# A decode block on one core: where 256 rows of w2 travel, and how the output sum is laid out in PSUM

## The chip, the core and the metric

The kernel runs on one core of a Trainium2 chip. Its metric is the device time of one execution in microseconds. The median of four runs is 134.85 us (134.83 to 134.93). The core has a matrix engine (TensorE, called PE in the profile; its weight loads are listed apart as PEld), a vector engine (DVE), a scalar engine (ACT), GpSimd (POOL) and SyncE (SP), which here issues most of the transfers. Sixteen DMA engines carry the transfers from HBM to the on-chip memory (SBUF). PE writes its results to PSUM, from which DVE and ACT read them.

## What is computed

One token for each of two batch rows (B = 2, Sq = 1, width D = 576) goes through an attention block over a window of the caches and, beside it, through a two-layer block with a squared ReLU. Both results are added to the input. With Hq = 32 query heads, Hkv = 16 key heads, head size 128, a cache of 8192 positions and F = 4608:

```
W = min(4096, max(256, Sk // 4))          # 2048 positions
q = (x @ wq) -> [B, Hq, 1, 128]
scores = q . k[last W] * 128**-0.5 ;  p = softmax(scores) ;  o = p . v[last W]
A = o.reshape(B, 1, Hq*128) @ wo
h = xn @ w1 + b1 ;  r = max(h, 0) ;  Bout = (r*r) @ w2 + b2
out = x + A(xn) + Bout(xn)                # xn = layernorm(x)
```

All inputs and the output are bf16. An execution reads 53.62 MB from HBM, nearly all of it caches and weights, and writes 2304 bytes.

## The kernel before

The work is cut into 8 units (4 groups of four key heads, 2 batch rows). For each unit, PE transposes the keys, forms scores, and later multiplies with the values; DVE and ACT copy transposed keys out of PSUM and make the softmax. `step(u)` interleaves the transposes and scores of unit u with the value product of unit u − 2. The products with `wo` (`wo_acc`), the hidden layer (`mlp_h_block`, `mlp_h_end`) and the products with `w2` (`mlp_o`, `mlp_x`, `mlp_tail`) follow by the order of the program text: PE's instructions are kept in program order.

SP's queue carries all large transfers, in this order: the first keys, `wq`, then keys and values in turn, the first half of `wo`, `w1`, the last two value tiles, the second half of `wo` (`issue_wo`, L156), and `w2` (`issue_w2`, L164). A transfer with 128 rows is shared out to the 16 DMA engines, 8 rows each. The keys, the values and the first three `w2` tiles take turns in six buffers (`kvpool`).

`w2` has 4608 rows. The first three quarters of 1152 rows each are one tile of 9 blocks of 128 rows. Of the last quarter, 7 blocks (896 rows) come last in SP's queue, as three transfers of 4, 2 and 1 blocks (`W2P`, L510). The other 256 rows travel early on ACT's queue in small transfers, one or two at a time (`issue_w2x`, L181), called from `load_k` and `load_v`. `XS` (L74) says how they are cut: each entry is (rows of w2 on a partition, partitions, partitions of one transfer). Before, 96 rows go as 4 transfers of 8 partitions with 3456 bytes each, and 160 rows as 4 transfers of 5 partitions with 9216 bytes each. `mlp_x` (L491) multiplies them by the hidden values.

The output sum is kept in PSUM. `out_ps` (L265) has two groups of 288 columns, group i on the partitions from 32 i on; each batch row lies on one partition of a group (16 apart). `out_acc` (L268) issues two matmuls of 288 columns for a block of rows. The sum starts with x and b2 (L556), and takes in the first `wo` half (L571), the 256 early rows (L580), the second `wo` half (L583) and three quarters of `w2` (L584). Then DVE and ACT copy it to SBUF (`part`, L586 to L589) in four pieces of 144 columns. The last 7 blocks go to another PSUM tile, `tail_ps`, in four column groups of 144 columns (`mlp_tail`, L479), four matmuls to a block. One DVE addition of `tail_ps` and `part` gives `fin_sb` (L594), and ACT issues its transfer to HBM (L595). Matmuls are recorded at L107 and transposes at L110, the lines of two helpers.

Of the kernel before, what the change touches and what calls it, by code (L numbers as in the profile page):

```python
# [8 lines left out]
F32 = mybir.dt.float32  # L9
BF16 = mybir.dt.bfloat16  # L10
ACT = mybir.ActivationFunctionType
ALU = mybir.AluOpType
# [4 lines left out]
def kernel(  # L17
# [14 lines left out]
    nc = tc.nc  # L32
    P = 128
    B, Sq, D = A_x.shape
# [32 lines left out]
    NG4 = 4  # L67
# [3 lines left out]
    HW = F // NG4  # L71
    HB = HW // 3
    FR = HW // P
    XS = ((3, 32, 8), (8, 20, 5))  # L74
    FT = (HW - sum(r * p for r, p, _ in XS)) // P
    F3 = (NG4 - 1) * HW
    CX = [(r, FT, P) for r in range(FT)]
    FX = []
    for xr, xp, _ in XS:
        FX.append(F3 + FT * P + sum(m * n for m, n, _ in XS[:len(FX)]))  # L80
        CX += [(FX[-1] - F3 + r, xr, xp) for r in range(xr)]
    assert FX[-1] + XS[-1][0] * XS[-1][1] == F
    N3 = (NG4 - 1) * FR
# [2 lines left out]
    BS = 16  # L86
    MB = BS * (B - 1) + 1
    RM = 32 * (NG4 - 1) + MB
    OH = D // 2
    OQ = D // 4  # L90
    NP = NQ // 2
    WR = 2 * NC * Dh // P
# [3 lines left out]
    const = ctx.enter_context(tc.tile_pool(name="const", bufs=1))  # L96
# [7 lines left out]
    psum = ctx.enter_context(tc.tile_pool(name="psum", bufs=1, space=bass.MemoryType.PSUM))  # L104

    def matmul(*a, **k):
        tc.keep_in_program_order(nc.tensor.matmul(*a, **k))  # L107
# [7 lines left out]
    k_tiles, v_tiles, wq_tiles, w1_tiles, wo_tiles, w2_tiles = {}, {}, {}, {}, {}, {}  # L115
# [59 lines left out]

    const.tile([P, 96], F32, name="pad_0")
    w2x_sb = [const.tile([xp, xr * D], BF16, name=f"w2x_sb_{i}") for i, (xr, xp, _) in enumerate(XS)]
    const.tile([P, 24], F32, name="pad_1")
    x_parts = [(s, i) for s, (_, xp, xe) in enumerate(XS) for i in range(xp // xe)]

    def issue_w2x():  # L181
# [61 lines left out]
    for sg in range(S):  # L243
# [12 lines left out]
                          in_=own[:].unsqueeze(2).to_broadcast([P, NC, HQ // NC]))  # L256
    in_s = const.tile([P, NS], F32, name="in_s")
    nc.vector.tensor_reduce(out=in_s[:], in_=ident[:].rearrange("p (g s c) -> p s g c", s=NS, c=NC), axis=AX.XY,
                            op=ALU.add)
    far_h = const.tile([TH, P], BF16, name="far_h")  # L260
    nc.vector.tensor_scalar(out=far_h[:].rearrange("p (a h r) -> p a h r", h=TH, r=rep),
                            in0=ident[0:TH, 0:TH].unsqueeze(1).unsqueeze(3).to_broadcast([TH, P // NC, TH, rep]),
                            scalar1=BIG, scalar2=-BIG, op0=ALU.mult, op1=ALU.add)
    is_h = ident[0:TH, 0:TH].unsqueeze(1).to_broadcast([TH, NJJ * 32 // TH, TH])
    out_ps = psum.tile([32 + MB, OH], F32, tag="out", name="out_ps")  # L265
    nc.vector.memset(out_ps[:], 0.0)

    def out_acc(lhsT, rhs_of, start=False, stop=False):  # L268
        for i in range(2):
            matmul(out_ps[32 * i:32 * i + MB, :], lhsT=lhsT, rhs=rhs_of(i * OH, (i + 1) * OH),  # L270
                   start=start, stop=stop, skip_group_check=True)

    QZ = 2 * NC
    qz = const.tile([P, NQ, B, 2, 3 * QZ], BF16, name="qz")
# [150 lines left out]
    def wo_acc(tq):  # L425
        ws = wo_state.pop(tq)
        wo_sb = wo_tiles.pop(tq)
        for r in range(WR):
            out_acc(ws[:, r, :], lambda a, z: wo_sb[:, r, a:z])

    mlp = {}
# [38 lines left out]
    def mlp_o(g, r0, r1):  # L470
        w2_sb = w2_tiles.pop((g, r0))
        for r in range(r0, r1):
            o = (r - r0) * D
            out_acc(mlp["h"][:, g * FR + r, :], lambda a, z: w2_sb[:, o + a:o + z], stop=(g == NG4 - 2 and r == r1 - 1))

    part = const.tile([RM, OQ], F32, name="part")
    nc.gpsimd.memset(part[:], 0.0)

    def mlp_tail(r0, r1):  # L479
        w2_sb = w2_tiles.pop((NG4 - 1, r0))  # L480
        if r0 == 0:
            mlp["out"] = psum.tile([P, OQ], F32, tag="o", name="tail_ps")
            nc.vector.memset(mlp["out"][:], 0.0)
        for r in range(r0, r1):
            o = (r - r0) * D
            for i in range(4):
                matmul(mlp["out"][32 * i:32 * i + MB, :], lhsT=mlp["h"][:, (NG4 - 1) * FR + r, :],
                                 rhs=w2_sb[:, o + i * OQ:o + (i + 1) * OQ], start=(r == 0), stop=(r == FT - 1),
                                 skip_group_check=True, tile_position=(0, 32 * i))

    def mlp_x():  # L491
        i = FT
        for w, (xr, xp, _) in zip(w2x_sb, XS):
            for r in range(xr):
                out_acc(mlp["h"][0:xp, N3 + i, :], lambda a, z: w[:, r * D + a:r * D + z])
                i += 1
# [13 lines left out]
    W2P = [(0, 0, 9), (1, 0, 9), (2, 0, 9), (3, 0, 4), (3, 4, 6), (3, 6, 7)]  # L510
# [33 lines left out]
    for t in range(NT):  # L544
# [7 lines left out]
                          in_=ident[0:NG4, 0:NG4].unsqueeze(2).to_broadcast([NG4, NG4, 32]))  # L552
# [28 lines left out]
    pv_all(NU - 1)  # L581
    wo_sel(1)
    wo_acc(1)  # L583
    for w in W2P[:NG4 - 1]:  # L584
        mlp_o(*w)
    for i in range(4):  # L586
        cp = nc.scalar.copy if i // 2 else nc.vector.tensor_copy
        cp(out=part[32 * i:32 * i + MB, :],  # L588
           in_=out_ps[32 * (i // 2):32 * (i // 2) + MB, (i % 2) * OQ:(i % 2 + 1) * OQ])  # L589
    for w in W2P[NG4 - 1:]:  # L590
        mlp_tail(*w[1:])

    fin_sb = work.tile([RM, OQ], BF16, tag="fin", name="fin_sb")
    nc.vector.tensor_tensor(out=fin_sb[:], in0=mlp["out"][0:RM, :], in1=part[:], op=ALU.add)  # L594
    nc.scalar.dma_start(out=out2d.rearrange("b (q n) -> q b n", q=4), in_=fin_sb[0:RM:BS, :])  # L595


# [28 lines left out]
```

## Time and profile before

| what | value |
|---|---|
| median of four runs | 134.85 us |
| the profiled execution | 134.87 us, of which its span 133.1 us |
| mean clock granted to PE | 0.858 of full speed |
| DMA | 53.74 MB at a mean 404 GB/s |
| instructions of PE, PEld, DVE, ACT, POOL | 850, 850, 160, 65, 18 |
| queues | q1: SP's large transfers; q10: ACT's small ones; q8 and q14: instructions |

The span runs from the first to the last instruction of the core; 1.8 us of the execution's time lie around it. A group or timeline line gives start or busy time, engine, source line, operation, the tile written and the tiles read, shapes and counts; the bracket at its end is the idle time of the engine before it, with what ended it. A line of the windows gives, for one stretch of time, the busy microseconds and instruction counts of PE, PEld, DVE, ACT and POOL, the clock granted to PE, the mean busy share of the 16 DMA engines, and GB/s. The chain of waits is followed back from the last instruction, at each step to what released it. The ends of matmuls are modelled in this profile.

### The profile page before, as it was taken

How to read it: one execution, taken by the hardware profiler on the slowest of the kernel's cores; microseconds unless marked ns; L12 is line 12 of the kernel's file. 1: busy time of each engine (PE TensorE's matmuls, PEld its weight loads, DVE VectorE, ACT ScalarE, POOL GpSimd, SP SyncE). 2: the span in 40 equal slices, each digit the busy share in tenths (PEclk: the TensorE clock that was granted, in tenths of full speed). 3: DMA queues.
4: the chain of work that ended last, by engine and by line, in shares of the span. 5: the costliest groups of instructions: out<-in, count | busy, mean ns of one | idle time of the engine just before them, and what ended most of it. 6: DMA issues, size and time to landing. Idle time of an engine off the chain costs nothing.

```text
span 133.1 us, 2082 instructions
## 1 busy us (share of the span) xinstructions
PE 90.7 (68%) x850; PEld 54.2 (41%) x850; DVE 58.7 (44%) x160; ACT 46.9 (35%) x65; POOL 5.4 (4%) x18
## 2 busy tenths in 40 slices
PE   0069746968597378569497599779755485927980
PEld 0059314544363235336253346536422243314650
DVE  6724405263484564484467537457520423061010
ACT  5715503078284255165085154366120400000010
POOL 7000000010100100100100100010100000000000
PEclk9999995599999999999999757999998555555599
DMA  3999999999999999999999999999999999999940
GB/s 119 432 412 422 443 414 453 414 438 424 419 433 442 419 446 409 448 414 449 409 438 428 424 443 424 438 416 443 438 418 427 414 456 426 422 412 433 407 187 1
DMA packets 4458, 53.74 MB, mean 404 GB/s; under 512 B 551, under 2 KB 682, under 8 KB 1230
## 3 DMA queue, kind: packets, MB, share of 16 engines
q1 hardware_dynamic: 4320, 53.32, 94.3%
q10 hardware_dynamic: 130, 0.31, 0.6%
q8 instruction: 6, 0.10, 0.3%
q14 instruction: 2, 0.02, 0.0%
HBM read 53.62 MB, written 0.00 MB: 403 GB/s over the span
## 4 chain that ended last, share of the span: by engine, by line
DMA 92%; PE 3%; DVE 1%; SPq 1%; issue 0%; DVEq 0%
DMA v<-in_A_v_cache_dram 43%; DMA k<-in_A_k_cache_dram 20%; DMA w<-in_B_w_dram 17%; DMA wq<-in_A_wq_dram 12%; PE kT_ps L110 2%; PE o_ps L107 1%; SPq L128 0%; DVE kT L329 0%; SPq L135 0%; DVE o L386 0%; DVE o L388 0%; DVE fin_sb L594 0%; PE tail_ps L107 0%; DVEq L594 0%
## 5 line engine op out<-in xcount | busy, mean ns | idle before, releaser
L110 PE MATMUL kT_ps<-ident_f,k 128*128 128x128 f32 x256 | 41.3, 307 | 12.1 <-DMA k<-in_A_k_cache_dram 7.9
L110 PEld LDWEIGHTS kT_ps<-ident_f,k 128*128 128x128 f32 x256 | 32.2, 157 | 26.3 <-issue 12.0
L327 ACT COPY kT<-kT_ps 128x1024 bf16<-128x1024 bf16 x32 | 31.8, 1012 | 22.2 <-PE kT_ps L110 22.1
L329 DVE COPY kT<-kT_ps 128x1024 bf16<-128x1024 bf16 x32 | 21.8, 683 | 16.8 <-PE kT_ps L110 16.5
L107 PE MATMUL sc_ps<-kT,qz 128*32 128x512 bf16 x128 | 10.5, 414 | 5.8 <-DVE kT L329 5.8
L107 PE MATMUL o_ps<-v,pT 128*32 128x512 bf16 x128 | 12.0, 474 | 0.3 <-DMA v<-in_A_v_cache_dram 0.3
L359 ACT ACTIVATE p<-sc_ps,bias 128x512 bf16<-128x512 f32 x8 | 5.5, 687 | 17.9 <-DVE gown L355 17.9
L588 ACT COPY part<-out_ps 17x144 f32<-17x144 f32 x2 | 0.5, 268 | 24.4 <-DVE part L588 24.4
L348 DVE TENSOR_REDUCE m<-sc_ps 128x1 f32<-128x512 f32 x8 | 5.5, 692 | 7.2 <-PE sc_ps L107 7.2
L388 DVE SCALAR_TENSOR_TENSOR o<-o_ps,in_s,o 128x128 f32<-128x128 f32 x24 | 8.3, 347 | 0.5
L362 DVE STREAM_TRANSPOSE pT<-p 128x512 bf16<-128x512 bf16 x8 | 5.7, 710 | 6.4 <-ACT p L359 6.4
L386 DVE TENSOR_SCALAR o<-o_ps,in_s 128x128 f32<-128x128 f32 x8 | 2.7, 341 | 10.8 <-PE o_ps L107 10.8
L107 PE MATMUL out_ps<-wo,ws 128*17 128x288 bf16 x64 | 6.1, 364 | 1.6 <-DVE ws L421 1.6
L352 POOL PARTITION_ALL_REDUCE gmax<-m x8 | 2.9, 365 | 90.2 <-DVE m L350 90.2
L107 PE MATMUL op_ps<-o,of_h 128*128 128x129 f32 x16 | 4.0, 340 | 3.3 <-DVE o L388 3.2
L107 PEld LDWEIGHTS <-qz 128*32 128x32 bf16 x128 | 2.2, 98 | 10.0 <-DVE kT L329 7.4
L107 PEld LDWEIGHTS <-hT_sb 128*17 128x17 bf16 (+2 forms) x104 | 4.8, 105 | 3.5 <-issue 0.9
L107 PEld LDWEIGHTS <-xnT 128*2 128x2 bf16 x100 | 2.3, 85 | 9.5 <-issue 8.1
L107 PEld LDWEIGHTS <-ws 128*17 128x17 bf16 x64 | 3.6, 112 | 3.8 <-DVE ws L421 1.8
L110 PE MATMUL pro_ps<-ident,tmp_x 2*128 2x2 bf16 x6 | 0.5, 176 | 6.6 <-DVE tmp_x L233 6.6
L107 PEld LDWEIGHTS op_ps<-o,of_h 128*128 128x128 f32 x16 | 2.8, 220 | 5.4 <-DVE o L388 5.4
L107 PE MATMUL h_ps<-w,xnT 128*2 128x384 bf16 x48 | 2.7, 363 | 3.2 <-DMA w<-in_B_w_dram 3.2
(79 smaller groups left out, 58.2 us busy)
## 6 DMA issues: line engine op xcount, KB each, us to landing
k<-in_A_k_cache_dram SPq DMA_DIRECT2D x8, 2048.0 KB, 23.5
v<-in_A_v_cache_dram SPq DMA_DIRECT2D x8, 2048.0 KB
wo<-in_A_wo_dram SPq DMA_DIRECT2D x2, 2304.0 KB
w<-in_B_w_dram SPq DMA_DIRECT2D x2, 2304.0 KB
wq<-in_A_wq_dram SPq DMA_DIRECT2D x2, 2048.0 KB, 16.4
w<-in_B_w_dram SPq DMA_DIRECT2D x3, 1296.0 KB
w_rem<-in_B_w_dram SPq DMA_DIRECT2D x1, 576.0 KB, 36.6
w<-in_B_w_dram SPq DMA_DIRECT2D x1, 576.0 KB
```

The source lines that it names most:

```text
L107: tc.keep_in_program_order(nc.tensor.matmul(*a, **k))
L110: tc.keep_in_program_order(nc.tensor.transpose(*a, **k))
L327: nc.scalar.copy(out=kT, in_=kT_ps[:])
L329: nc.vector.tensor_copy(out=kT, in_=kT_ps[:])
L348: nc.vector.tensor_reduce(out=m1[:], in_=sc_ps[:], axis=AX.X, op=ALU.max)
L352: nc.gpsimd.partition_all_reduce(gmax[:], m2[:], channels=P, reduce_op=ReduceOp.max)
L359: nc.scalar.activation(out=p_sb[:], in_=sc_ps[:], func=ACT.Exp, bias=bias[:, 0:1], scale=scale, accum_out=o1[:, Dh:Dh + 1])
L362: nc.vector.transpose(out=pT[:].rearrange("p j r -> p (j r)"), in_=p_sb[:])
L386: nc.vector.tensor_scalar(scalar1=in_s[:, 0:1], scalar2=None, op0=ALU.mult, **kw)
L388: nc.vector.scalar_tensor_tensor(scalar=in_s[:, k:k + 1], in1=o1[:, 0:Dh], op0=ALU.mult, op1=ALU.add, **kw)
L588: cp(out=part[32 * i:32 * i + MB, :], in_=out_ps[32 * (i // 2):32 * (i // 2) + MB, (i % 2) * OQ:(i % 2 + 1) * OQ])
```

## The change

The 256 early rows are cut in another way. The 160 rows in transfers of 5 partitions with 9216 bytes stay and now come first; the other 96 rows become one transfer of 96 partitions with 1152 bytes each, which is shared out to all DMA engines. So ACT issues five such transfers in place of eight, and `mlp_x` has 9 blocks in place of 11.

`out_ps` now has four column groups of 144 columns from the start, and `out_acc` issues four matmuls of 144 columns for a block of rows. All blocks of `w2`, the last seven too, go through `mlp_o` into this one tile. `mlp_tail`, `tail_ps`, `part` and its four copies go away. One ACT copy takes the whole of `out_ps` to `fin_sb`. A padding tile in SBUF grows by 384 bytes on each partition.

```diff
-    XS = ((3, 32, 8), (8, 20, 5))
+    XS = ((8, 20, 5), (1, 96, 96))
...
-    const.tile([P, 24], F32, name="pad_1")
+    const.tile([P, 120], F32, name="pad_1")
...
-    out_ps = psum.tile([32 + MB, OH], F32, tag="out", name="out_ps")
+    out_ps = psum.tile([RM, OQ], F32, tag="out", name="out_ps")
     nc.vector.memset(out_ps[:], 0.0)
 
     def out_acc(lhsT, rhs_of, start=False, stop=False):
-        for i in range(2):
-            matmul(out_ps[32 * i:32 * i + MB, :], lhsT=lhsT, rhs=rhs_of(i * OH, (i + 1) * OH),
-                   start=start, stop=stop, skip_group_check=True)
+        for i in range(4):
+            matmul(out_ps[32 * i:32 * i + MB, :], lhsT=lhsT, rhs=rhs_of(i * OQ, (i + 1) * OQ), start=start, stop=stop,
+                   skip_group_check=True, tile_position=(0, 32 * i))
...
-            out_acc(mlp["h"][:, g * FR + r, :], lambda a, z: w2_sb[:, o + a:o + z], stop=(g == NG4 - 2 and r == r1 - 1))
-
-    part = const.tile([RM, OQ], F32, name="part")
-    nc.gpsimd.memset(part[:], 0.0)
-
-    def mlp_tail(r0, r1):
-        w2_sb = w2_tiles.pop((NG4 - 1, r0))
-        if r0 == 0:
-            mlp["out"] = psum.tile([P, OQ], F32, tag="o", name="tail_ps")
-            nc.vector.memset(mlp["out"][:], 0.0)
-        for r in range(r0, r1):
-            o = (r - r0) * D
-            for i in range(4):
-                matmul(mlp["out"][32 * i:32 * i + MB, :], lhsT=mlp["h"][:, (NG4 - 1) * FR + r, :],
-                                 rhs=w2_sb[:, o + i * OQ:o + (i + 1) * OQ], start=(r == 0), stop=(r == FT - 1),
-                                 skip_group_check=True, tile_position=(0, 32 * i))
+            out_acc(mlp["h"][:, g * FR + r, :], lambda a, z: w2_sb[:, o + a:o + z], stop=(g == NG4 - 1 and r == FT - 1))
...
-    for w in W2P[:NG4 - 1]:
+    for w in W2P:
         mlp_o(*w)
-    for i in range(4):
-        cp = nc.scalar.copy if i // 2 else nc.vector.tensor_copy
-        cp(out=part[32 * i:32 * i + MB, :],
-           in_=out_ps[32 * (i // 2):32 * (i // 2) + MB, (i % 2) * OQ:(i % 2 + 1) * OQ])
-    for w in W2P[NG4 - 1:]:
-        mlp_tail(*w[1:])
 
     fin_sb = work.tile([RM, OQ], BF16, tag="fin", name="fin_sb")
-    nc.vector.tensor_tensor(out=fin_sb[:], in0=mlp["out"][0:RM, :], in1=part[:], op=ALU.add)
+    nc.scalar.copy(out=fin_sb[:], in_=out_ps[:])
```

More of the change, by code (lines that the diff above doesn't have):

```diff
@@ L88 @@
     RM = 32 * (NG4 - 1) + MB
-    OH = D // 2
     OQ = D // 4
```

## The prediction

> **What bounds the kernel now.** I read the page first, then the chain of waits in order of time, the windows of the last microseconds, the timeline of the same stretch, and the records of single DMA packets under them (each with queue, size, start and duration).
>
> ```profile
> PE 90.7 (68%) x850; PEld 54.2 (41%) x850; DVE 58.7 (44%) x160; ACT 46.9 (35%) x65; POOL 5.4 (4%) x18
> ...
> q1 hardware_dynamic: 4320, 53.32, 94.3%
> q10 hardware_dynamic: 130, 0.31, 0.6%
> q8 instruction: 6, 0.10, 0.3%
> ...
> DMA 92%; PE 3%; DVE 1%; SPq 1%; issue 0%; DVEq 0%
> ```
>
> No compute engine is above 68%. The DMA engines carry 92% of the chain, and the DMA row of the page is at 9 tenths from the second slice to the thirty-eighth.
>
> ```profile
> 107.64 22.06 DMA w<-in_B_w_dram
> 129.70 0.04 issue
> 129.74 0.27 PE tail_ps L107 x4
> ...
> 130.08 0.31 DVE fin_sb L594
> ```
>
> This is the end of the chain: the last w2 transfer, four matmuls, one addition. The transfer does not end on all 16 DMA engines together:
>
> ```profile
> 127.70:128.20 0.50, 0.50 (x14) 0.39 (x10) 0.00 (x0) 0.00 (x0) 0.00 (x0) 1.00 0.62 238
> 128.20:128.70 0.50, 0.43 (x12) 0.12 (x10) 0.08 (x1) 0.00 (x0) 0.00 (x0) 1.00 0.38 141
> 128.90:129.20 0.30, 0.18 (x12) 0.03 (x1) 0.29 (x2) 0.00 (x0) 0.00 (x0) 1.00 0.13 46
> 129.20:129.40 0.20, 0.04 (x4) 0.04 (x7) 0.03 (x1) 0.06 (x1) 0.00 (x0) 1.00 0.07 23
> ```
>
> The last two columns are the DMA share and GB/s. 0.13 is two engines of 16, 0.07 is one. So the bound is the most loaded DMA engine, not the bytes. Chained by start and end, the packet records give 16 engines. They finish their w2 work between 126.53 and 129.40 us, and their order follows what else each carried:
> - no extra packet: about 126.5 to 127.0;
> - a q8 packet (16 KB of instructions, 0.88 to 0.97 us each): six engines, 128.0 to 128.6;
> - four w2x packets of 9216 B and four of 3456 B, which the change's wording calls engines 0 to 4: 128.52, 128.62, 128.77, 129.22 and 129.40. The last two also carry a q14 packet of 8 KB.
>
> For the last engine, start, extra packets and slow packets add up to 129.39, against 129.40 recorded.
>
> **The change part by part.**
>
> *The w2x rows.* On one engine a 3456 B packet takes 131 ns from start to start, a 1152 B packet 47, the closing 4 B write 5. Engines 0 to 4 keep the 9216 B packets, lose four transfers of one 3456 B packet (4 x 136 = 544 ns) and gain one share of the 96-row transfer (6 x 47 + 5 = 287): −0.257 us. Engines 5 to 7 change alike; engines 8 to 15 gain 0.287. The latest of those without 9216 B packets ends at 128.59, so at most at 128.88 after. The five become 128.26, 128.36, 128.52, 128.96 and 129.14. The last landing moves from 129.40 to 129.14. Bounds: −0.44 (if the other loads let 128.96 be last) and 0 (if some other load takes the gain back). I take −0.26, since the sum of the packets explains the last engine within 0.01 us.
>
> *Output in four column groups.* Per block of rows, two matmuls of 288 columns become four of 144.
>
> ```profile
> 120.51 4.01 PE L107 MATMUL out_ps<-wo,ws 128*17 128x288 bf16 x32 [1.55 <-DVE ws L421]
> ...
> 124.32 4.26 PE L107 MATMUL out_ps<-w,hT_sb 128*17 128x288 bf16 x54
> ...
> 128.65 0.43 PE L107 MATMUL tail_ps<-w,hT_sb 128*17 128x144 bf16 x16
> ```
>
> The tail already has the new form: four blocks start 62.5 ns apart at clock 1.00. In the old form blocks start 122 ns apart at clock 1.00 and 240 at 0.50, so I estimate the new form at 125 at 0.50. w2x goes from 11 blocks (2.64 us) to 9 (1.1), the second wo part from 4.0 to 2.0, each w2 tile of 9 blocks to 1.1. One w2 tile takes 8 x 385.5 ns = 3.08 us to arrive, so each is summed before the next is there: PE, now done at 128.58, waits on every landing instead. None of this is on the path; worth 0, as the last matmuls wait for the last landing before and after.
>
> The Trainium skill ("TensorEngine Tiling (Array Packing)", Instruction Overhead) speaks against more and smaller matmuls: about 60 cycles for each. By that rule the 134 added matmuls would be about 3.4 us at 2.4 GHz (an estimate from the page), still under the spare 2 us of each w2 tile; the tail's 16 matmuls in 0.43 us do not show it.
>
> *The clock at the end.* The clock came back from 0.50 to 1.00 at 125.92, after a window with PE busy throughout:
>
> ```profile
> 119.09:122.50 3.41, 1.99 (x18) 1.22 (x20) 1.26 (x4) 0.00 (x0) 0.00 (x0) 0.50 1.00 426
> 122.50:125.92 3.42, 3.42 (x32) 2.04 (x30) 0.00 (x0) 0.00 (x0) 0.00 (x0) 0.50 0.99 417
> ```
>
> With half the work PE is busy about 1.1 us of each 3.08, so I expect 0.50 to the end. A 288-column matmul at the head of a group took 282 ns at 1.00 and 412 at 0.50; 144 columns fewer is 60 ns less of that difference, so the last four matmuls take 0.07 longer: +0.07 (0 if the clock returns; above, +0.16, the growth of a queued one, 286 to 448).
>
> *One ACT copy.* The addition on DVE took 0.307 and began 0.103 after PE's end, as it waits for PE and for ACT's part copies (a separate waiting instruction, then the addition). The copy waits for PE alone; ACT copies after PE began 0.036 to 0.048 later. The part copies on ACT took 0.268 for the same 144 columns on 17 partitions, and I take that for 113, as 98 and 128 partitions of 1024 columns both took 1.012. Together −0.06 − 0.04 = −0.10. The output transfer follows DVE by 0.033 now; following ACT's own completion I take the same, between 0 and +0.1. It is queued on ACT behind the copy alone, and its other wait is for a transfer that landed long before.
>
> *Hidden or empty.* The four part copies (0.30 each on DVE, 0.27 on ACT) end at 129.88, under the wait for the last matmuls: 0. Two memsets go (0.22 on POOL at 2.8 us, 0.18 on DVE at 118.2): 0, under the DMA stream. ACT issues five w2x transfers instead of eight (0.63 to 0.76 each); their completions share a rotation of eight with SP's, and SP now waits on three of them. From SP's waits (us in total, times, longest):
>
> ```profile
> SPq L128 <- DMA w2x_sb<-in_B_w_dram: 16.2, 3, 14.1
> ```
>
> and the page's table of DMA issues (its last column is the time from issue to landing):
>
> ```profile
> k<-in_A_k_cache_dram SPq DMA_DIRECT2D x8, 2048.0 KB, 23.5
> ```
>
> A k transfer lands 23.5 us after its issue, so SP is several transfers ahead: moving these waits costs 0 unless that lead is used up. SP's order of transfers is unchanged. The early 9216 B packets delay engines 0 to 4 by 0.42 at about 6 us, under the same lead.
>
> *More instructions.* PE gets 264 more. The six q8 packets start about every 250 PE records (matmuls and weight loads), so one more is due, 0.9 us on one engine, while w2 arrives. Four of the six lie on engines without w2x packets, two on engines 5 to 7, each on another one; if the seventh goes to the next, it meets an engine at 126.5 to 127.0, which then ends near 128.2, hidden. The Trainium skill ("Runtime: NRT & Kernel Launch", Instruction fetch mechanics) says blocks of 16 KiB, 256 instructions, mostly hidden; it does not name the DMA engine.
>
> Sum against the profiled execution (134.87; span 133.1 and 1.8 around it; 0.02 above the median of 134.85): −0.26 − 0.10 + 0.07 = −0.29, 134.58 there, 134.56 against the median.
>
> **The rivals.**
> 1. The last engine does not move: slow packets at the start (they add up to 1.0 us on the last engine, 0.1 on the least) fall differently and eat 0.26. For: that spread. Against: runs within 0.1 us of each other. −0.10 + 0.07: 134.82.
> 2. Slower: the seventh instruction packet lands on one of engines 0 to 4. On the one ending at 129.14 it gives 130.06: +0.66 − 0.10 + 0.07 = +0.63, 135.48. It costs more than the rest gains from the engine now at 128.77 upwards, three of the five. Against: the six packets avoid these five.
> 3. PE becomes the bound: were the four groups to take turns, a block at 0.50 would be 480 ns, a w2 tile 4.3 us against 3.08 of arrival, and three tiles end about 4 us late: 138.5. Against: the tail's rows.
> 4. More gain: the clock is back at 1.00 (134.49), or a q14 packet falls elsewhere and 128.96 is last: 134.38.
>
> **How the numbers follow.** The sum as forecast has 0.55 (134.45 to 134.70), rival 1 0.17, rival 2 0.11, rival 3 0.03, rival 4 0.14. The range leaves out rivals 2 and 3 and a part of the edges: 134.36 to 134.92. A difference under 0.2% (0.27 us) is about what a measurement of this kernel can't tell from none, and the forecast lies at that edge, 134.58: faster takes two thirds of the first case and all of rival 4 (0.50), within 0.2% the rest of it and nearly all of rival 1 (0.34), slower rivals 2 and 3 with a tail of 1 (0.16).
>
> **What would show it.** In the windows the last DMA share goes to zero at about 129.14 instead of 129.40; the output sums show three separate bursts of 36 matmuls with waits for w2 between; the clock is 0.50 in the last windows; the copy starts under 0.05 after PE and takes 0.27; q8 counts 7 packets. The prediction is wrong if the DMA share lasts beyond 129.3, if PE is still busy with a w2 tile when the next lands, or if the copy or the output transfer waits for something else.

## The result and the profile after

The changed kernel takes 134.75 us (median; 134.55 to 134.89) against 134.86 (134.76 to 135.18) for the kernel before on the same chips. The ratio is 0.9989 with a 95% interval of 0.9984 to 0.9993, so 0.15 us less, between 0.09 and 0.22. That is a real gain, but within 0.2%. The forecast of 134.56 lies 0.19 below the median; the range from 134.36 to 134.92 holds it. Some executions of kernels below took longer, up to 140.6 us, and in the three of these that were traced the 16 KB packets were 0.07 us slower over part of the run; the ratios leave out executions from 136.9 us up, the ranges given show them all.

The profiled execution of the changed kernel took 134.55 us, at the lower edge of its spread, while the one of before, at 134.87, lay in the middle of its own. So the two traces differ by 0.32 us, twice what the ratio gives. This matters below: the trace after shows what the change can do, and other executions have to show what it does as a rule.

From the page after (the span; engines with busy time, share and instructions; DMA queues with packets, MB and share of 16 engines):

```profile
span 132.8 us, 2335 instructions
PE 86.0 (65%) x982; PEld 52.5 (40%) x982; DVE 57.2 (43%) x156; ACT 46.6 (35%) x64; POOL 5.2 (4%) x17
...
q1 hardware_dynamic: 4320, 53.32, 94.6%
q10 hardware_dynamic: 178, 0.31, 0.6%
q8 instruction: 7, 0.11, 0.3%
```

PE has more instructions and less busy time. The small queue q10 carries the same bytes in more packets, and there is a seventh instruction packet on q8.

The end of the chain of waits after (start, duration, what):

```profile
101.19 27.20 DMA w<-in_B_w_dram
128.39 0.04 issue
128.43 0.66 PE out_ps L106 x16
129.09 0.04 issue
129.13 0.71 PE out_ps L106 x12
129.84 0.02 issue
129.86 0.28 ACT fin_sb L572
```

The addition on DVE is gone; one ACT copy follows PE by 0.046 us (from the unrounded records). The x12 group from 129.13 hides the last wait inside it: its last four matmuls wait for the last landing, as the windows after show (the last two columns are the DMA share and GB/s, the one before them the clock granted to PE):

```profile
127.70:128.20 0.50, 0.50 (x21) 0.40 (x13) 0.00 (x0) 0.00 (x0) 0.00 (x0) 0.50 0.75 284
128.20:128.70 0.50, 0.37 (x16) 0.27 (x15) 0.00 (x0) 0.00 (x0) 0.00 (x0) 0.50 0.42 152
...
128.90:129.20 0.30, 0.26 (x12) 0.07 (x7) 0.00 (x0) 0.00 (x0) 0.00 (x0) 0.50 0.07 23
129.20:129.40 0.20, 0.20 (x8) 0.14 (x8) 0.00 (x0) 0.00 (x0) 0.00 (x0) 0.50 0.00 0
```

Nothing moves after 129.20; before, one engine was still busy in the last of these stretches. The clock is 0.50 to the end, where it was 1.00. The timeline after shows why:

```profile
118.88 2.10 PE L106 MATMUL out_ps<-wo,ws 128*17 128x144 bf16 x64 [1.55 <-DVE ws L420]
120.85 1.26 PE L106 MATMUL out_ps<-w,hT_sb 128*17 128x144 bf16 x36
123.94 1.26 PE L106 MATMUL out_ps<-w,hT_sb 128*17 128x144 bf16 x36 [1.83 <-DMA w<-in_B_w_dram]
127.04 2.77 PE L106 MATMUL out_ps<-w,hT_sb 128*17 128x144 bf16 x64 [1.84 <-DMA w<-in_B_w_dram]
129.86 0.28 ACT L572 CAST fin_sb<-out_ps 113x144 bf16<-113x144 f32 x1 [24.56 <-PE out_ps L106]
```

A `w2` tile of nine blocks is summed in 1.26 us, and PE then waits 1.8 us for the next one. Before, PE ran through this stretch without a pause.

The path of the end can be split by the records of packets, matmuls and completions. All values are in us; "landing" is the end of the last packet of the last `w2` transfer (PE is released about 0.3 later), "issue" is when ACT starts to issue the output transfer, and what lies around the span is the time less the span.

| execution | landing | to issue | issue to span's end | around the span | time |
|---|---|---|---|---|---|
| before | 129.40 | 1.03 | 2.66 | 1.79 | 134.87 |
| after | 129.17 | 1.00 | 2.59 | 1.79 | 134.55 |
| difference | −0.23 | −0.03 | −0.07 | 0 | −0.32 |

### The profile page after: what moved, and what is told of

Its sections match the earlier page's. It is cut to its first block, busy times and chain, and to the rows that moved or that the text cites. A ratio compares the mean times of both kernels' runs of the same rounds, so it can differ in the third digit from the quotient of the medians.

```text
span 132.8 us, 2335 instructions
## 1 busy us (share of the span) xinstructions
PE 86.0 (65%) x982; PEld 52.5 (40%) x982; DVE 57.2 (43%) x156; ACT 46.6 (35%) x64; POOL 5.2 (4%) x17
## 4 chain that ended last, share of the span: by engine, by line
DMA 77%; PE 16%; SPq 2%; DVE 2%; issue 1%; ACT 0%; DVEq 0%
DMA w<-in_B_w_dram 47%; DMA k<-in_A_k_cache_dram 17%; DMA wq<-in_A_wq_dram 13%; PE kT_ps L109 8%; PE sc_ps L106 3%; PE q_ps L106 2%; PE o_ps L106 1%; PE out_ps L106 1%; DVE qrow L292 1%; SPq L127 1%; SPq L134 1%; PE qT_ps L109 1%; DVE kT L328 1%; DVE qz L308 0%; SPq L158 0%
## 5 line engine op out<-in xcount | busy, mean ns | idle before, releaser
L109 PE MATMUL kT_ps<-ident_f,k 128*128 128x128 f32 x256 | 39.8, 300 | 11.0 <-DMA k<-in_A_k_cache_dram 7.7
L109 PEld LDWEIGHTS kT_ps<-ident_f,k 128*128 128x128 f32 x256 | 30.7, 152 | 25.2 <-issue 11.6
L106 PEld LDWEIGHTS <-xnT 128*2 128x2 bf16 x100 | 2.8, 100 | 12.9 <-issue 12.1
L106 PE MATMUL out_ps<-w,hT_sb 128*17 128x144 bf16 x136 | 5.1, 319 | 3.8 <-DMA w<-in_B_w_dram 3.7
L106 PE MATMUL h_ps<-w,xnT 128*2 128x384 bf16 x48 | 3.2, 421 | 5.8 <-DMA w<-in_B_w_dram 5.8
L452 DVE TENSOR_TENSOR hrow<-t 98x384 bf16<-98x384 f32 x3 | 1.6, 557 | 8.3 <-ACT t L451 8.2
L106 PE MATMUL q_ps<-wq,xnT 128*2 128x512 bf16 x32 | 2.7, 477 | 3.2 <-DMA wq<-in_A_wq_dram 3.2
```

Of the source, the lines that this page charges most:

```text
L109: tc.keep_in_program_order(nc.tensor.transpose(*a, **k))
L452: nc.vector.tensor_tensor(out=hrow[:, k * HB:(k + 1) * HB], in0=t1, in1=t1, op=ALU.mult)
```

## The experiments

**1. Each part alone.** The first kernel takes the new cut of the rows into the kernel before:

```diff
-    XS = ((3, 32, 8), (8, 20, 5))
+    XS = ((8, 20, 5), (1, 96, 96))
...
-    const.tile([P, 24], F32, name="pad_1")
+    const.tile([P, 616], F32, name="pad_1")
```

> Only the new cut of the 256 early rows, on the kernel before. First theory: the end follows the DMA engine that lands last, and the cut takes 0.26 us from it: about 134.60, last landing near 129.14 in the trace, clock back at 1.00 at the end. Rival A (the column groups or the ACT copy cost more than the 0.03 gain that was forecast for them together): the same 134.60 here. Rival B (the gain of the rows is itself eaten in most executions, by loads on the DMA engines that differ from one execution to the next): about 134.75, with a wider spread than the kernel before.

Measured: 134.67 us (134.53 to 134.82), ratio 0.9984 (0.9976 to 0.9993), so −0.21 us between −0.32 and −0.09. The end of its chain of waits:

```profile
107.38 22.08 DMA w<-in_B_w_dram
129.46 0.04 issue
129.50 0.27 PE tail_ps L107 x4
129.77 0.04 DVEq L594
129.80 0.05 issue
129.85 0.31 DVE fin_sb L594
```

Before, the same chain had the four matmuls at 129.74, so they move by 0.24. The end keeps its old form: four matmuls in 0.27, then the addition, 1.03 us from landing to issue. The rows alone bring the whole gain. Part of it, 0.08, lies behind the issue of the output: from there to the span's end it is 2.58 in this trace, where it was 2.66.

The second kernel has the four column groups and the ACT copy with the old cut of the rows:

```diff
-    XS = ((8, 20, 5), (1, 96, 96))
+    XS = ((3, 32, 8), (8, 20, 5))
...
-    const.tile([P, 120], F32, name="pad_1")
+    const.tile([P, 168], F32, name="pad_1")
```

> Only the four column groups and the ACT copy, with the old cut of the early rows. First theory and rival B: 0.10 less after the last matmul, 0.07 more for the slower clock, so 134.83, last landing at 129.40 as before. Rival A: 134.97 or more, as the whole change gained some 0.15 less than forecast.

Measured: 135.08 us (134.78 to 136.04), ratio 1.0026 (1.0008 to 1.0044): slower by 0.35 us, and not by what lies on the path. The landing of its trace, 129.36, and the 1.00 us to issue are as forecast, but the time around the span was 1.78 to 3.04 us from execution to execution, where it is 1.8 in the kernels above. This cost does not appear in the changed kernel, so it needed a cause of its own (experiment 4).

**2. The whole change again, and before again.** The changed kernel ran beside the two parts, which gave a second trace of it; then each kernel ran once more, for a third trace of the changed one and a second of the one before.

> The changed kernel once more, for a second trace. First theory: the same order of engines as in the first trace, last landing 129.17, time within 0.05 of 134.55. Rival B: a time nearer to 134.75, and a last landing later by the same amount, with a load on the last engine that the first trace does not show there.

Measured: 134.70 us (134.53 to 134.82), ratio 0.9987 (0.9978 to 0.9995). On the same chip the rows alone took 134.67, so the groups and the copy add nothing that shows. Its last landing was at 129.20.

> The changed kernel, a third trace. The two traces so far are of executions at 134.55 and 134.61, the median is 134.70 to 134.75. First theory: the last landing between 129.15 and 129.35, on an engine that carries four packets of 9216 B and one 8 KB instruction packet, and the time 5.4 us after it. Rival B: another engine last, or another load on it.

> The kernel before, a second trace. First theory: last landing near 129.40, on an engine with the same packets as in its first trace. Rival B: a last landing that differs from the first by 0.1 us or more, with slow packets at the start to account for it.

Measured: 134.91 us for the changed kernel and 134.89 for the one before. The second trace of before repeats the first: landing 129.40, 1.03 to issue. The third trace of the changed kernel does not repeat its first; its windows are

```profile
128.90:129.20 0.30, 0.30 (x16) 0.30 (x11) 0.00 (x0) 0.00 (x0) 0.00 (x0) 0.50 0.09 31
129.20:129.40 0.20, 0.20 (x11) 0.04 (x1) 0.00 (x0) 0.00 (x0) 0.00 (x0) 0.50 0.06 23
129.40:129.60 0.20, 0.17 (x12) 0.11 (x8) 0.00 (x0) 0.00 (x0) 0.00 (x0) 0.50 0.03 12
```

and the end of its chain is

```profile
129.48 0.70 PE out_ps L106 x12
130.18 0.02 issue
130.21 0.28 ACT fin_sb L572
```

One engine is at work until 129.52, 0.35 later than in the first trace after (129.17), and the time is 0.36 longer. Everything behind the landing is the same: 0.99 to issue, 2.60 from there. So the difference between these traces is that of the last landing; in the second trace, too, the landing (129.20) and the time (134.61) lie 0.03 and 0.06 above the first. The packet records of the engine that ends last show a stall of 295 ns right behind its second 9216 B packet, at 9.37 us. No such stall stands on the last engine in the first trace after. The stall is not the whole difference: added up packet by packet, this engine is 0.27 later than in the first trace by 12 us, and it loses another 0.07 between 50 and 56 us, where the packets of the 96-row transfer lie. In the run of the rows alone, the second-last engine stalls for 209 ns at the same place, at 9.95 us; in the two traces of before, whose packets there have 3456 B, the largest single stall is 132 ns. But in the second of them the losses between 8 and 12 us add up to 0.22 on each of the last two engines, so losses there do not come with 9216 B packets alone.

**3. The same rows at another time, and in other cuts.** If the early 9216 B packets cost time on engines 0 to 4, sending them later should recover it. Here the first two calls of `issue_w2x` send nothing. All five transfers move by this: the first 9216 B packets leave at about 31 us instead of 5.6, and the 96-row transfer travels at 59 to 63 us instead of 50 to 55:

```diff
+    x_calls = []
+
     def issue_w2x():
-        if x_parts:
+        x_calls.append(0)
+        if x_parts and len(x_calls) > 2:
             s, i = x_parts.pop(0)
```

> The changed kernel with the first two early-row transfers issued later: the calls at the start of the program issue nothing, so the first 9216 B packets come at about 32 us instead of 5.6 and 9 us. Theory C, from three traces of the changed kernel (last landing 129.17, 129.20, 129.52): in some executions the packets next to the early 9216 B ones stall for 0.2 to 0.7 us at 9 to 11 us, on the very engines that end last, and that takes back a part of the 0.26. Then: last landing near 129.15 in nearly every execution, median about 134.58, spread narrower than 0.3. Rival: the stalls at the start come anyway and fall on other packets: 134.70, spread as before.

Measured: 134.52 us (134.45 to 134.70, and one execution of 140.2), ratio 0.9977 (0.9968 to 0.9986), so −0.31 us between −0.43 and −0.19. Every execution but that one has a span of 132.7 to 132.9. Windows and end of the chain:

```profile
128.90:129.20 0.30, 0.25 (x12) 0.15 (x8) 0.00 (x0) 0.00 (x0) 0.00 (x0) 0.50 0.04 12
129.20:129.40 0.20, 0.20 (x8) 0.06 (x1) 0.00 (x0) 0.00 (x0) 0.00 (x0) 0.50 0.00 0
```

```profile
102.44 26.57 DMA w<-in_B_w_dram
129.00 0.04 issue
129.05 0.71 PE out_ps L106 x10
129.75 0.02 issue
129.78 0.28 ACT fin_sb L575
```

The last landing is at 129.08. This kernel is faster than both. It gains 0.16 us more than the change did (0.31 − 0.15), with an uncertainty of about 0.14 from the two intervals, so the difference is shown, but not its exact size, and not which of the moved transfers brings it. The early packets are one candidate; what they do at 9 to 11 us is read from single traces, and in this one the last engine loses nothing there, but neither does it in the first two traces of the changed kernel. The 96-row transfer is the other. On the engine that ends last it took longer than its own packets need, by 0.09, 0.14 and 0.16 us in the three traces of the changed kernel and by 0.08 with the rows alone; here, at 59 to 63 us, by 0.02. No run moved one without the other.

The next kernel spreads all but 80 of the rows over all engines, which gives many small packets:

```diff
-    XS = ((8, 20, 5), (1, 96, 96))
+    XS = ((8, 10, 5), (1, 96, 96), (1, 80, 80))
...
```

> The changed kernel with 80 rows on engines 0 to 4 (two transfers of 5 partitions) and 176 rows on all (one transfer of 96 partitions, one of 80). Engines 0 to 4 lose two packets of 9216 B (696 ns) and all engines gain five packets of 1152 B (240 ns). First theory: the last landing comes from an engine with an instruction packet, 128.54 + 0.24 = 128.78 against 129.17 in the profiled execution of the changed kernel: about 0.39 less, 134.36 where the median of the changed kernel is 134.75. If the engines without w2x packets of 9216 B had been last in most executions already (a form of rival B), it is 0.1 to 0.25 slower than the changed kernel.

Measured: 135.04 us (134.75 to 138.3), ratio 1.0012 (1.0001 to 1.0023): a loss where the load of engines 0 to 4 alone would give a gain. Three things showed. The last landing of its trace is at 129.46, and between 9 and 11 us engines 0 to 4 have 16 KB packets that are slow by 194, 370, 298 and 236 ns and a 9216 B packet that is slow by 424. While the two spread transfers travelled, from 32 to 44 us, every engine without an instruction packet lost 0.2 to 0.3 us beyond its own packets. And the time around the span varied from 1.74 to 3.6 us, as in the groups alone.

The even cut has no packet that only some engines carry:

```diff
-    XS = ((8, 20, 5), (1, 96, 96))
+    XS = ((2, 128, 128),)
...
```

> The changed kernel with all 256 early rows in one transfer of 128 partitions with 2304 B, 8 packets on each DMA engine (8 x 89 + 5 = 720 ns), and no packet that only engines 0 to 4 carry. In the second trace of the changed kernel the two last engines (129.20) carry four packets of 9216 B and an 8 KB instruction packet each; the next ones (128.5 to 128.6) a 16 KB instruction packet. First theory (the load on the last engine sets the end): engines 0 to 4 end at 129.20 - 1.39 - 0.29 + 0.72 = 128.24, those with 16 KB at 128.59 - 0.29 + 0.72 = 129.02: last landing 0.18 earlier than in the changed kernel, about 134.52. Rival B (loads that differ from one execution to the next decide, and fall on any engine): no gain, 134.70 or more, as with the spread over 96 and 80 partitions, whose five engines with 9216 B packets fell behind by up to 0.7 us at 9 to 11 us of the run.

Measured: 134.71 us (134.56 to 134.75), ratio 0.9989 (0.9981 to 0.9998). The last landing, 129.05, is early, and now the engines that carried a 16 KB instruction packet end last (128.92 and 129.05). But from landing to the last block's first matmul it took 0.465 instead of 0.34 us, and from issue to the span's end 2.77 instead of 2.59; the two eat the gain. Why these two grew is open.

**4. The time around the span.** The groups alone and the spread rows have longer PE programs than the changed kernel (1699 and 1689 instructions against 1679, counted in the program; the PE and PEld records of a trace add up to 285 more in each kernel). To see whether the length itself does it, eight matmuls of two columns are added to the changed kernel near its start, which makes 1695:

```diff
+    pad_ps = psum.tile([P, 2], F32, tag="sc", bufs=2, name="pad_ps")
+    for i in range(8):
+        matmul(pad_ps[:], lhsT=ident[:], rhs=ident[:, 0:2], start=True, stop=True)
```

> The changed kernel with 8 added matmuls of 2 columns at the start, where PE waits for the first keys: 16 more PE instructions, 1695 in place of 1679. Theory D: in the runs so far the time outside the span is 1.79 for programs with 1403, 1415, 1609 and 1679 PE instructions and 1.8 to 3 in most executions of those with 1689, 1695 and 1699; a block of 256 instructions ends between, and the end of PE's program waits for one more block. Then: spans as in the changed kernel (132.7 to 133.0), time minus span 1.8 to 2.6, median 134.85 to 135.1. Rival: the time outside the span has another cause in those kernels: 134.70, 1.79.

Measured: 134.78 us (134.57 to 140.63), ratio 1.0006 (0.999 to 1.0023). The spans stay at 132.7 to 132.9 in all executions but two; the time around them is 1.75 to 2.57. The counter-test makes the groups alone shorter, with 1667 instructions. It leaves 80 of the 160 rows out of the sum, though all of them are loaded:

```diff
...
-            for r in range(xr):
+            for r in range(min(xr, 4)):
                 out_acc(mlp["h"][0:xp, N3 + i, :], lambda a, z: w[:, r * D + a:r * D + z])
                 i += 1
+            i += xr - min(xr, 4)
```

> The four column groups and the ACT copy with the old cut, as in the run of the groups alone, but 80 of the 160 rows are left out of the sum (4 blocks of matmuls, 32 PE instructions: 1667 in place of 1699); all rows are still loaded. Theory D: time minus span is 1.79 in every execution, and what is left is the groups' own effect, -0.03 by the forecast: 134.80 against 134.83. Rival A (the groups cost time by themselves): 134.95 or more, with 1.79 outside the span or not.

Measured: 134.89 us (134.79 to 135.07), ratio 1.0005 (0.9996 to 1.0013), and 1.74 to 1.84 us around the span in every execution. So most of the loss of the groups alone was the length of the PE program, not the groups. In all kernels here, those of up to 1679 instructions keep 1.8 us and those from 1689 do not always. The packet records show what comes with the length. In the traces of the four kernels with 1689 to 1699 instructions queue q8 carries an eighth 16 KB packet; in those of all shorter programs it carries six or seven. In three of the four it starts 0.9 to 1.0 us behind the span's end, with 1.90 to 1.97 us around the span. In the fourth (experiment 5) it starts at 131.67, inside the span, with 1.79 around it. The executions with more than 2 us around the span have no trace.

The four groups with their copy are worth +0.07 us, between −0.05 and +0.18: no gain shown, and the forecast of −0.03 not excluded.

**5. The clock at the end.** Four matmuls of 512 columns after each of the first two `w2` tiles keep PE busy, so that the clock may return:

```diff
     for w in W2P:
+        w2_full = w2_tiles[w[:2]]
         mlp_o(*w)
+        if w[0] < 2:
+            fill_ps = psum.tile([P, 512], F32, tag="kT", bufs=3, name=f"fill_{w[0]}")
+            for i in range(4):
+                matmul(fill_ps[:], lhsT=ident[:], rhs=w2_full[:, 512 * i:512 * (i + 1)], start=True, stop=True)
```

> The changed kernel with four added matmuls of 512 columns (into a PSUM tile that nothing reads) after each of the first two w2 tiles, while PE waits for the next tile; they use rows that are already there. First theory: PE is busy without a gap from 118.9 to about 125, so the clock goes back to 1.00 and the last four matmuls take 0.23 in place of 0.30: 0.07 less, 134.63 where the changed kernel has 134.70, with the last landing unchanged. If the clock at the end costs nothing, no difference; if the added matmuls hold up the w2 tiles, up to 0.5 more.

Measured: 134.88 us (134.52 to 136.15), ratio 1.0015 (0.9997 to 1.0034). The windows of its trace, one of the longer executions, with the last landing at 130.77:

```profile
123.90:125.30 1.40, 0.73 (x3) 0.26 (x3) 0.00 (x0) 0.00 (x0) 0.00 (x0) 1.00 1.01 430
...
128.40:130.00 1.60, 0.74 (x36) 0.59 (x36) 0.00 (x0) 0.00 (x0) 0.00 (x0) 1.00 0.65 251
130.00:131.50 1.50, 1.09 (x28) 0.58 (x27) 0.00 (x0) 0.04 (x1) 0.00 (x0) 0.65 0.05 19
```

The clock came back to 1.00, and a whole `w2` tile took 0.74 instead of 1.26 us. This alone does not need the added matmuls. In the second trace of the changed kernel the second `w2` tile ran in 0.74, too, and the third in 1.26 again, at 0.50:

```profile
123.98 0.74 PE L106 MATMUL out_ps<-w,hT_sb 128*17 128x144 bf16 x36 [2.02 <-DMA w<-in_B_w_dram]
127.08 2.78 PE L106 MATMUL out_ps<-w,hT_sb 128*17 128x144 bf16 x64 [2.36 <-DMA w<-in_B_w_dram]
```

The third trace and that of the late transfers show the same. With the added matmuls the clock held through the third tile as well. But PE was then idle for most of 127.0 to 128.4 us, and the clock fell before the last matmuls, which ran at 0.50 again and took 0.298 us. This PE program, too, is longer than the changed kernel's (1695 instructions), and the time around the span reached 2.6 us. The run says nothing on the price of the last matmuls at 1.00 in this form. The rule of the Trainium skill ("TensorE: Matmul & The Clock Gate", Part 1) that activity within a window of some 3.4 us releases the throttle, and idleness sets it again, agrees with these rows, but not with this one of the kernel before:

```profile
112.26:115.68 3.42, 3.42 (x34) 1.56 (x32) 0.00 (x0) 0.00 (x0) 0.00 (x0) 0.50 0.99 424
```

PE was busy throughout, and the clock stayed at 0.50 until 125.92. So a busy window was not always enough, and what decides it was not tested here.

**6. Both ideas together.** Fewer rows on engines 0 to 4, sent late, with a PE program of 1649 instructions:

```diff
-    XS = ((8, 20, 5), (1, 96, 96))
+    XS = ((4, 20, 5), (1, 96, 96), (1, 80, 80))
...
-        if x_parts:
+        x_calls.append(0)
+        if x_parts and len(x_calls) > 2:
...
```

> A version from the findings: the changed kernel with 80 rows on engines 0 to 4 in packets of 4608 B (four transfers of 5 partitions, 4 rows on each), 176 rows on all engines in packets of 1152 B, nothing issued at the start, and 1649 PE instructions. First theory with C and D: last landing from an engine with a 16 KB instruction packet, 128.59 + 0.24 = 128.83, or from one of engines 0 to 4, 129.20 - 4 x 348 + 4 x 179 + 0.24 = 128.76: about 0.37 before the changed kernel, 134.30, outside the span 1.79. If the spread over more packets costs as much as in the run with 96 and 80 partitions, 134.75 or more.

Measured: median 134.52 us, ratio 0.9987 (0.9966 to 1.0008): ten executions at 134.33 to 134.71 and four at 136.1 to 140.4. Its lowest time, 134.33, is the lowest of all kernels here, but the comparison is unclear, and its trace is of one of the long executions (span 138.2), so it shows nothing on the landing.

## Where the prediction was right, and where it was wrong

**The bound.** Right. The last DMA engine sets the end. Between the first and the third trace of the changed kernel a landing 0.35 later made the time 0.36 longer.

**The w2x rows, −0.26.** The mechanism was right, and the size in the trace after nearly so: the five engines with 9216 B packets ended at 128.20, 128.31, 128.35, 128.96 and 129.17, for a forecast of 128.26, 128.36, 128.52, 128.96 and 129.14. As a rule it is less. The whole change gave −0.15 where the sum had −0.29, and the traces of the changed kernel have about 0.09 of it behind the landing. That leaves about 0.06 for the landing itself, as an estimate from these two numbers; reckoned alike, the rows alone have 0.13 and the late transfers 0.22. So this is the likeliest term to have been mis-sized. The missing 0.14 can't be split with certainty, as the rows alone gave −0.21 (−0.32 to −0.09) and the groups' +0.07 is known only within 0.12.

Two costs that the sum put at nothing stand in the packet records of the last engine. The first belongs to the sentence "The early 9216 B packets delay engines 0 to 4 by 0.42 at about 6 us, under the same lead." The lead covers SP and the other engines, but an engine that ends last has no cover: of what it loses at 9 us nothing is won back by 129, as the third trace shows, where it was 0.27 behind the first by 12 us. The second belongs to the 287 ns for the 96-row transfer, which count its own packets alone: on the last engine it took 80 to 160 ns more. Sending all these transfers later brought the median to 134.52, for a forecast of 134.56. How much each of the two costs in a typical execution was not shown.

**One ACT copy, −0.10, and the clock, +0.07.** Right within 0.02 as a sum. The gap behind PE went from 0.103 to 0.046 (forecast about 0.04), the work from 0.307 to 0.280 (0.268), the last four matmuls from 0.242 to 0.301 (+0.06 for +0.07). The three together are −0.025 on the path in the first trace after, −0.03 forecast. That the clock would be 0.50 to the end held for the last matmuls of every trace with the new end; before them it was back at 1.00 for a tile or two in some. And the reading that it came back before "after a window with PE busy throughout" leaves out the window from 112.26, just as busy, which did not bring it back.

**Four column groups, 0.** Right: three separate bursts of 36 matmuls with waits between them, PE no bound. Rival 3 is out.

**More instructions, 0.** Right for the seventh packet: it came at 124.61 us, on an engine without 9216 B packets, which ended at 128.54, so rival 2 is out. The Trainium skill ("Runtime: NRT & Kernel Launch", Instruction fetch mechanics) calls such loads mostly hidden; here they are hidden only as long as another engine ends later, and in the even cut they were the last. What the forecast had not seen is the cost outside the span: the changed kernel stands ten PE instructions under the length of the shortest program here that shows it and that carries an eighth packet.

**Not forecast at all: −0.07 from issue to the span's end** (2.66 to 2.59). It goes with this cut of the rows (2.58 with the rows alone, 2.71 to 2.72 with the old cut and the groups, 2.65 and 2.77 with the spread and the even cut); the cause is open. Without it the median would be near 134.82, where rival 1 stands: this part of the agreement with the forecast is luck.

**The rivals.** The median of 134.75 is nearer to rival 1 (134.82) than to the sum, and outside the likeliest case's own 134.45 to 134.70. Rival 1 named slow packets at the start as what could eat the gain; it was given 0.17, argued against from runs of before that lie within 0.1 us of each other. Those runs had 3456 B packets where the change puts 9216 B ones, so they were no evidence on this. Slow packets at the start are what the third trace shows; the 96-row transfer, which no rival named, stands beside them. Rival 4 is out: the clock was 0.50 at the end, and the two q14 packets fell on two of the five engines again.

## What to carry to other kernels

Where DMA engines set the end, add up each engine's own packets, stalls and instruction loads: a small transfer on the engine that ends last costs its full time, however early it is sent, and no lead of a queue covers it. A transfer that is spread over all engines can cost that engine more than its own packets. Send such transfers on engines that have slack, or not at the crowded start, and measure the place as well as the size. When a change makes an engine's program longer, look at the time around the span too, and at the packets behind the span's end, since no view inside the span shows it.

## What the runs showed that was not expected

- In every trace of a kernel with 9216 B packets that was followed packet by packet, the last two engines are those of the five with 9216 B packets that also carry one of the two 8 KB packets of q14 (one at about 31 to 33 us, one at 60 to 71). That packet takes 0.305 us, and the 16 KB packet behind it is slow by 0.53 to 0.59 us for the first and 0.24 to 0.42 for the second. A 16 KB packet behind an instruction packet of q8 was slow by 0.47 to 0.55 us in the same way, where it was seen.
- Stalls of 0.2 to 0.4 us stand beside the second 9216 B packets at 9 to 11 us in some traces and not in others. Why was not found.
- The 96-row transfer of 1152 B packets took 0.08 to 0.16 us more on the last engine than its own packets when it travelled at 50 to 55 us, and 0.02 at 59 to 63 us. Why was not found.
- A PE program of 1689 to 1699 instructions made the time around the span vary up to 3.6 us, where it is 1.8 up to 1679 instructions. An eighth 16 KB instruction packet goes with it.
- From the issue of a 2304 B output to the span's end it took 2.58 to 2.77 us, by kernel, with the same last instructions.
